# Both softmaxes moved ahead of the transposes' copies on ACT, in a top-k attention followed by a GELU MLP

## The chip, the core and the metric

The kernel runs on one core of a Trainium2 chip, in float32. The core has five engines, each with its own instruction queue that it works through in order: PE (matrix products and transposes through the identity), ACT (activations and copies out of PSUM), DVE (vector work, here the top-k search), POOL (elementwise work) and SP (issues DMAs). Matmul results go to PSUM, which has eight banks per partition; everything else lies in SBUF. An engine that reaches an instruction whose input is not there, or whose output buffer is still in use, stands still, and everything behind it in its queue stands too.

The metric is the device time of one execution in microseconds. Less is better.

## What is computed

For 8 batches of 8 heads with 576 positions of 64 elements: scores, the 32 largest of each row kept, softmax over them, product with v. The result, seen as 4608 tokens of 512 elements, goes through an MLP with an exact GELU (512 to 2048 to 512).

```python
scores = scale * np.matmul(q, k.transpose(0, 1, 3, 2))
kth = np.partition(scores, -top_k, axis=-1)[..., -top_k:-top_k + 1]
scores = np.where(scores >= kth, scores, -1000000000.0)
scores = scores - np.max(scores, axis=-1, keepdims=True)
attn = np.exp(scores)
attn = attn / (np.sum(attn, axis=-1, keepdims=True) + 1e-09)
attn_out = np.matmul(attn, v)
...
h = x @ w_in
g = 0.5 * h * (1.0 + erf(h * inv_sqrt2))
return g @ w_out
```

## The kernel before

**Items.** Two heads are a pair. The 576 positions of a head are four blocks of 128 and a tail of 64. An item is one block of 128 query positions of both heads of a pair; the tails of two pairs together are one item too (`t == NM` in the code). There are 18 items a batch, 144 in all (`N`), and two batches, 36 items, are one round of the schedule.

**The pipeline.** The main loop (L689) has one iteration per item and keeps four items at different stages. In iteration `n`:

- `scores(n + 2)` (L277): eight matmuls into the PSUM tile `s_ps` (L293), for the first 512 keys of each head; one more into `t_ps` (L298) for the last 64 keys of both heads; ACT copies them to the SBUF row tile `s` (L306, L309). Tail items use L315, L326, L332 and L335.
- `top_k(n)` (L341): on DVE, for each of two heads four rounds of MAX8 (L355, the eight largest) with a MATCH_REPLACE8 between rounds (L358, takes them out). `hooks` lets another step run inside; here `inverse(n - 1)` after the fourth round's MAX8.
- `threshold(n)` (L366): on POOL, two tiny steps (L370, L373) turn the top values into the two biases of the softmax.
- `softmax(n - 1, e)` (L390), `e` being the head: on ACT, a Prelu with a huge slope pushes everything under the 32nd value far down (L394), then Exp, with the row sum gathered into `den` (L395).
- `add_small(n - 1)` (L384): POOL adds 1e-9 to `den` (L387). `inverse(n - 1)` (L378): DVE takes the reciprocal (L381). `normalise(n - 1)` (L401): POOL multiplies both rows by it (L407), on five items DVE does it.
- `transposes(n - 2)` (L417): PE transposes the 512 main columns of both heads into two PSUM tiles `tp` (L436), ACT copies them to `pt` (L448). The returned `tails` transposes the last 64 columns of both heads (L453, L458) into the spare half of `t_ps`; its copy is L454 or L465.
- `attend(n - 3)` (L482): PE multiplies by v (L500, L511) once two blocks of a pair are transposed, that is in every other iteration, and for every tail item; it returns whether there was a product. ACT copies the product `o` to `xT`, the MLP's input (L505, L515, run by `copy_x`).

**The MLP** is cut into pieces, placed into PE's queue by `mlp(k)` (L638), which puts in up to `k` of them. An iteration has a quota of eight (`left`), four in iterations 10 and 11; a w_in piece is only taken when its tokens are finished (`ready`, set behind `scores`). A w_in piece is four matmuls into `h_ps` (L552); two units of them are followed by their GELUs on ACT (L563). A w_out piece is two matmuls into `y_ps` (L588), copied by ACT and stored by SP. Blocks of eight w_in pieces and of eight w_out pieces alternate, so an iteration has one or the other. What is left when the 144 items are through runs as one block at the end.

**PSUM.** The tag `tp` has two banks for which `tp` (twice), `t_ps`, the q/k transposes `tp_qk` and `o` take turns. `s_ps` is single, and takes two banks; `h_ps` and `y_ps` have two each.

**Other work in the loop.** The transposes of q and k of later pairs (`transpose_qk`, L234) come in pieces that are laid into fixed iterations (`prep_in`); the first piece also issues the next loads of q and k on SP. Up to iteration 18 the weights arrive as 16 units and are put together by ACT (`weights_size`) and POOL (`weights_add`, `weights_end`). Before iteration 10 (`START`) there is no MLP to do, and `keep_busy` puts idle matmuls into PE's queue.

**The order** is written by hand (`manual_schedule`): each engine's queue is the order in which the Python code emits its instructions. In the steady part (`late`) an iteration emits: `attend`, `copy_x`, one MLP piece (two without a product), the transposes of item n-2, scores and last keys of item n+2 with the tail transposes, softmax of head 0, one piece, two pieces, softmax of head 1, `add_small`, the q/k pieces, the other MLP pieces, GELUs, then search, threshold and normalise.

Of the kernel before, what the change touches and what calls it, by code (L numbers as in the profile page):

```python
# [14 lines left out]
def kernel(  # L15
# [169 lines left out]
    def waits(u):  # L185

        return u == ORDER[-1]
# [80 lines left out]
    def half(r, e):  # L268


        return slice((r ^ e) * TL, ((r ^ e) + 1) * TL)
# [2 lines left out]

        return spread(t[:, e * TL :], step + (TL if e == 0 else -TL), TL)

    def scores(i, tails=None):  # L277

        if i >= N:
            if tails:  # L280
                t_ps = ps.tile([P, 512], f32, tag="tp", name="t_ps")
                tails(t_ps)()
            return
        pair, t = items[i]
        S_of[i] = s = work.tile([P, 2 * S], f32, tag="s", bufs=5, name="s")
        s_ps = ps.tile([P, 2, 512], f32, tag="s", bufs=1, name="s_ps")
        if t < NM:
            qk = qk_of[pair]
            lhsT = qk[:, t * P : (t + 1) * P]
            for c in range(2):  # L290
                for e in range(2):
                    rows = slice(e * D, (e + 1) * D)
                    nc.tensor.matmul(  # L293
                        s_ps[:, e, c * 256 : (c + 1) * 256], lhsT=lhsT[rows, :],
                        rhs=qk[rows, KT + c * 256 : KT + (c + 1) * 256], start=True, stop=True,
                    )
            t_ps = ps.tile([P, 512], f32, tag="tp", name="t_ps")
            nc.tensor.matmul(t_ps[:, 0:P], lhsT=lhsT, rhs=qk[:, SM + P : KT], start=True, stop=True)  # L298
            copy_tails = tails(t_ps) if tails else None
            if i == 0:  # L300

                nc.scalar.activation(s[:, 0:SM], s_ps[:, 0], func=AF.Copy, scale=scale)
                nc.vector.tensor_scalar(s[:, SM : S + TL], t_ps[:, 0:P], scale, None, op0=ALU.mult)
                nc.scalar.activation(s[:, S + TL :], s_ps[:, 1], func=AF.Copy, scale=scale)  # L304
                return
            nc.scalar.activation(spread(s, S + TL, SM), s_ps, func=AF.Copy, scale=scale)  # L306
            if copy_tails:
                copy_tails()
            nc.scalar.activation(s[:, SM : S + TL], t_ps[:, 0:P], func=AF.Copy, scale=scale)  # L309
        else:  # L310
            t_ps = ps.tile([P, 512], f32, tag="tp", name="t_ps")
            for r in range(2):
                qk = qk_of[pair + r]
                for e in range(2):
                    nc.tensor.matmul(  # L315
                        t_ps[half(r, e), r * TL : (r + 1) * TL],
                        lhsT=qk[:, SM + e * TL : SM + (e + 1) * TL],
                        rhs=qk[:, SM + P + e * TL : SM + P + (e + 1) * TL],
                        start=True, stop=True,
                    )  # L320

            for r in range(2):
                qk = qk_of[pair + r]
                for e in range(2):
                    rows = slice(e * D, (e + 1) * D)
                    nc.tensor.matmul(  # L326
                        s_ps[half(r, e), r, :], lhsT=qk[rows, SM + e * TL : SM + (e + 1) * TL],
                        rhs=qk[rows, KT:], start=True, stop=True,
                    )
            copy_tails = tails(t_ps) if tails else None  # L330
            s2 = s.rearrange("p (r n) -> p r n", r=2)
            nc.scalar.activation(s2[:, :, 0:SM], s_ps, func=AF.Copy, scale=scale)  # L332
            if copy_tails:
                copy_tails()
            nc.scalar.activation(  # L335
                s2[:, :, SM:S], t_ps[:, 0:P].rearrange("p (r n) -> p r n", r=2),
                func=AF.Copy, scale=scale,
            )

    def top_k(i, hooks):  # L340


        stat_of[i] = st = {
            "top": work.tile([P, 2, TOPK], f32, tag="top", name="top"),
            "neg": work.tile([P, 2, 2], f32, tag="neg", name="neg"),
            "bias": work.tile([P, 2], f32, tag="bias", name="bias"),
            "den": work.tile([P, 2], f32, tag="den", name="den"),
            "rden": work.tile([P, 2], f32, tag="rden", name="rden"),
        }
        cur = [row(i, e) for e in range(2)]  # L350
        rest = work.tile([P, 2, S], f32, tag="rest", bufs=1, name="rest")
        n_op = 0
        for r in range(TOPK // 8):
            for e in range(2):
                nc.vector.max(st["top"][:, e, 8 * r : 8 * r + 8], cur[e])  # L355
            if r < TOPK // 8 - 1:
                for e in range(2):
                    nc.vector.match_replace(  # L358
                        rest[:, e], st["top"][:, e, 8 * r : 8 * r + 8], cur[e], LOWEST
                    )  # L360
                cur = [rest[:, e] for e in range(2)]
            if r in hooks:
                hooks.pop(r)()

    def threshold(i):

# [16 lines left out]
    def add_small(i):  # L383
        if i < 0 or i >= N:  # L384
            return
        st = stat_of[i]
        nc.gpsimd.tensor_scalar(st["den"], st["den"], 1e-9, None, op0=ALU.add)  # L387

    def softmax(i, e):

        if i < 0 or i >= N:
            return
        st, s = stat_of[i], row(i, e)
        nc.scalar.activation(s, s, func=AF.Prelu, bias=st["neg"][:, e, 1:2], scale=1.0, alpha=STEEP)  # L394
        nc.scalar.activation(  # L395
            s, s, func=AF.Exp, bias=st["bias"][:, e : e + 1], scale=1.0,
            accum_out=st["den"][:, e : e + 1],
        )
# [75 lines left out]
    def copy_x():  # L474
        while copies:
            copies.pop()()
# [161 lines left out]
    def mlp(n):  # L638
        for _ in range(n):
            if done[0] >= len(pieces) or pieces[done[0]][0] > ready[0] or left[0] == 0:  # L640
                return
            pieces[done[0]][1]()
            done[0] += 1
            left[0] -= 1
            if eager[0]:
                run_gelus()
# [22 lines left out]
    for pair in range(2):  # L669
        for piece in transpose_qk(pair, pair == 0):  # L670
            piece()
        if pair == 0:
            scores(0)
            scores(1)

# [11 lines left out]
    for n in range(ahead):  # L689

        left[0] = 4 if n in (START, START + 1) else 8
        eager[0] = n > N
        if not waits(unit_in(n)):
            weights_add(unit_in(n))
        product = attend(n - 3)
        late = n > START
        if not late:

            softmax(n - 1, 0)
        copy_x()  # L700
        if waits(unit_in(n)):
            weights_size(unit_in(n))
            weights_add(unit_in(n))
        if not (product and late and done[0] < len(pieces) and pieces[done[0]][0] > ready[0]):
            mlp(1)
            if not product:
                mlp(1)
        if n < START:

            keep_busy((4 if product or n == 0 else 14) * (1 if n < 5 else 2), ident)  # L710

        scores(n + 2, transposes(n - 2))
        ready[0] = n_tok[0]
        if late:
            softmax(n - 1, 0)
        mlp(1)
        if not late:
            softmax(n - 1, 1)
        prep = prep_in.pop(n, [])
        if n == START + 1:  # L720

            for piece in prep:
                piece()
            prep = []
        if n < START and product:
            keep_busy(5 if n < 5 else 10, ident)
        mlp(2)
        if late:
            softmax(n - 1, 1)
        add_small(n - 1)  # L730
        if ends_late(unit_in(n)):
            weights_end(unit_in(n))
        for piece in prep:
            piece()
            mlp(1)
        if n == 1:
            keep_busy(8, ident)

        run_gelus()
        mlp(left[0])  # L740
        run_gelus()
        if n < N:
            top_k(n, {3: lambda: inverse(n - 1)})
        else:
            inverse(n - 1)
        threshold(n)
        u = unit_in(n + 1)

        normalise(n - 1, 2 if on_pool(u) else 0)

        if not waits(unit_in(n + 1)):
            weights_size(unit_in(n + 1))
        for m in (n + 1, n + 2):

            if m > 2 and waits(unit_in(m)) == (m == n + 1):
                load_weights(m)
        if n <= NP:
            load("v", n)
# [38 lines left out]
```

## Time and profile before

| | us |
|---|---|
| median of three runs | 1755.2 (1753.03 to 1757.11) |
| the profiled execution | 1757.0 |
| its span, first to last instruction | 1755.2 |
| PE busy | 1618.2 (92%) |
| DVE busy | 1419.1 (81%) |
| ACT busy | 1173.6 (67%) |
| PE's weight loads busy | 1073.1 (61%) |
| POOL busy | 665.3 (38%) |
| first search starts / last reciprocal / closing MLP from | 10.3 / 1676.6 / 1689.3 |

The mean clock granted to PE was 0.982 of full speed. ACT loads its function tables 136 times, at 1.283 us each, about once for Exp and once for Gelu in two iterations.

How to read the lines below. A line of the timeline has the start in us, the length in us, the engine and source line, the operation, what it writes and reads, and how many instructions were merged; in square brackets stands the idle time of the engine before it, and who ended it. A line of the chain of waits in order of time has start, length and what. A line of the list of waits has who waited for whom, the total in us, how often, and the longest.

### The profile page before, as it was taken

Reading aid. Unit: us, or ns where it says so; the run is one execution under the profiler, and the core shown is the slowest. Engines: PE = TensorE matmul, PEld = TensorE weight load, DVE = VectorE, ACT = ScalarE, POOL = GpSimd, SP = SyncE. Lnnn points to the kernel's source line nnn. Section 1 sums busy time; section 2 is a strip of 40 time slices with the busy share of each in tenths; the row PEclk is TensorE's granted clock in tenths of the full one; section 3 lists DMA queues with packets and bytes.
Section 4 is the critical chain, followed back from the end, with each engine's and each line's share of the span. In section 5 each row is a group of like instructions: output and inputs, shape, how many; then the busy total and the mean of one; then the engine's idle time right before and its main releaser. Section 6 shows DMA issues by size and latency. Waiting matters only on the chain.

```text
span 1755.2 us, 28033 instructions
## 1 busy us (share of the span) xinstructions
PE 1618.2 (92%) x10336; PEld 1073.1 (61%) x10336; DVE 1419.1 (81%) x3046; ACT 1173.6 (67%) x2132; POOL 665.3 (38%) x760
## 2 busy tenths in 40 slices
PE   7778989999999999999999989999999999999999
PEld 6566566666656556666666556666666655666565
DVE  7888888888888778888888878888888878888800
ACT  6777876777767666677777767667676766666630
POOL 4775753333333323333333333333333323333300
PEclk9889999999999999999999999999999999999999
DMA  5422320011100110001100111001110001000000
GB/s 153 130 73 78 97 64 1 13 27 34 40 1 27 28 28 27 1 27 34 28 26 11 30 28 40 1 13 27 41 33 1 26 15 33 1 13 3 5 13 12
DMA packets 126777, 56.34 MB, mean 32 GB/s; under 512 B 117776, under 2 KB 118064, under 8 KB 126640
## 3 DMA queue, kind: packets, MB, share of 16 engines
q1 hardware_dynamic: 125376, 54.12, 11.5%
q8 instruction: 82, 1.34, 0.3%
q10 hardware_dynamic: 1200, 0.39, 0.1%
q14 instruction: 55, 0.45, 0.1%
q0 software_dynamic: 64, 0.03, 0.0%
HBM read 45.08 MB, written 9.44 MB: 31 GB/s over the span
## 4 chain that ended last, share of the span: by engine, by line
PE 49%; ACT 30%; POOL 18%; issue 2%; DMA 1%; SPq 0%; POOLq 0%; ACTq 0%; DVE 0%; DVEq 0%
PE y_ps L588 22%; POOL s L407 14%; ACT s L395 7%; PE o L500 7%; PE h_ps L552 6%; ACT s L394 6%; PE tp L436 5%; ACT L395 5%; ACT s L306 4%; ACT pt L448 4%; PE s_ps L293 4%; PE t_ps L298 1%; PE s_ps L326 1%; PE warm L666 1%; POOL neg L370 1%
## 5 line engine op out<-in xcount | busy, mean ns | idle before, releaser
L355 DVE MAX8 top<-rest 128x8 f32<-128x576 f32 x864 | 609.3, 747 | 0.0
L552 PE MATMUL h_ps<-xT,w_in_sb 128*128 128x256 f32 (+1 forms) x2560 | 535.0, 362 | 8.5 <-ACT g L563 8.5
L588 PE MATMUL y_ps<-w_out_sb,g 128*128 128x512 f32 x1152 | 528.7, 598 | 0.0
L552 PEld LDWEIGHTS h_ps<-xT,w_in_sb 128*128 128x128 f32 x2560 | 438.2, 191 | 73.8 <-issue 13.4
L407 POOL TENSOR_SCALAR s<-s,rden 128x576 f32<-128x576 f32 x278 | 476.4, 1723 | 0.6 <-DVE rden L381 0.4
L358 DVE MATCH_REPLACE8 rest<-top,rest 128x576 f32<-128x576 f32 x576 | 423.3, 742 | 0.0
L387 POOL TENSOR_SCALAR den<-den 128x2 f32<-128x2 f32 x144 | 32.0, 222 | 965.6 <-ACT s L395 965.6
L448 ACT COPY pt<-tp 128x512 f32<-128x512 f32 x256 | 137.4, 589 | 353.9 <-PE tp L436 353.9
L588 PEld LDWEIGHTS y_ps<-w_out_sb,g 128*128 128x128 f32 x1152 | 212.9, 193 | 198.2 <-issue 194.8
L395 ACT ACTIVATE s<-s,bias 128x576 f32<-128x576 f32 x288 | 223.3, 775 | 12.9 <-ACT s L394 0.4
L381 DVE RECIPROCAL rden<-den 128x2 f32<-128x2 f32 x144 | 23.8, 166 | 249.7 <-POOL den L387 249.7
L436 PE MATMUL tp<-ident,s 64*128 64x64 f32 x2304 | 128.0, 236 | 102.6 <-POOL s L407 95.5
L394 ACT ACTIVATE s<-s,neg 128x576 f32<-128x576 f32 x288 | 222.2, 772 | 0.0
L436 PEld LDWEIGHTS tp<-ident,s 64*128 64x128 f32 x2304 | 94.1, 141 | 192.8 <-POOL s L407 158.1
L358 DVE MATCH_REPLACE8 rest<-top,s 128x576 f32<-128x576 f32 x288 | 211.7, 743 | 0.0
L355 DVE MAX8 top<-s 128x8 f32<-128x576 f32 x288 | 201.8, 742 | 0.1
L500 PE MATMUL o<-pt,raw_v 128*64 128x256 f32 x1280 | 152.9, 386 | 0.8 <-ACT s L309 0.8
L293 PE MATMUL s_ps<-qk 64*128 64x256 f32 x1024 | 145.2, 404 | 1.4 <-ACT s L304 0.8
L500 PEld LDWEIGHTS o<-pt,raw_v 128*64 128x64 f32 x1280 | 86.6, 137 | 83.9 <-issue 40.6
L306 ACT ACTIVATE s<-s_ps 128x1024 f32<-128x1024 f32 x127 | 130.0, 1024 | 7.7 <-PE s_ps L293 7.4
L563 ACT ACTIVATE g<-h_ps 128x512 f32<-128x512 f32 x144 | 78.6, 595 | 37.8 <-PE h_ps L552 37.1
L293 PEld LDWEIGHTS s_ps<-qk 64*128 64x128 f32 x1024 | 92.4, 196 | 9.1 <-ACT s L304 1.0
(77 smaller groups left out, 1173.7 us busy)
## 6 DMA issues: line engine op xcount, KB each, us to landing
raw_q<-in_q_dram SPq DMA_DIRECT2D x64, 128.0 KB, 2.4
raw_v<-in_v_dram SPq DMA_DIRECT2D x64, 128.0 KB, 2.4
raw_k<-in_k_dram SPq DMA_DIRECT2D x62, 128.0 KB, 2.4
out_dram<-y SPq DMA_DIRECT2D x31, 256.0 KB, 2.2
w_out_sb<-in_moe_w_in_dram SPq DMA_DIRECT2D x14, 511.8 KB, 5.1
w_out_sb<-in_moe_w_out_dram SPq DMA_DIRECT2D x10, 511.8 KB, 4.1
words<-in_moe_w_out_dram SPq DMA_DIRECT2D x6, 511.8 KB, 4.3
out_dram<-y SPq DMA_DIRECT2D x9, 128.0 KB, 2.4
```

The source lines that it names most:

```text
L293: nc.tensor.matmul(s_ps[:, e, c * 256 : (c + 1) * 256], lhsT=lhsT[rows, :], rhs=qk[rows, KT + c * 256 : KT + (c + 1) * 256], start=True, s ...
L306: nc.scalar.activation(spread(s, S + TL, SM), s_ps, func=AF.Copy, scale=scale)
L355: nc.vector.max(st["top"][:, e, 8 * r : 8 * r + 8], cur[e])
L358: nc.vector.match_replace(rest[:, e], st["top"][:, e, 8 * r : 8 * r + 8], cur[e], LOWEST)
L394: nc.scalar.activation(s, s, func=AF.Prelu, bias=st["neg"][:, e, 1:2], scale=1.0, alpha=STEEP)
L395: nc.scalar.activation(s, s, func=AF.Exp, bias=st["bias"][:, e : e + 1], scale=1.0, accum_out=st["den"][:, e : e + 1],)
L407: (nc.vector if e >= 2 - on_dve else nc.gpsimd).tensor_scalar(s, s, st["rden"][:, e : e + 1], None, op0=ALU.mult)
L436: nc.tensor.transpose(tps[g][:, at : at + TL], s[rows, first[e] + j * P : first[e] + (j + 1) * P], ident[rows, rows],)
L448: nc.scalar.copy(out=dst, in_=src)
L500: nc.tensor.matmul(o[e * D : (e + 1) * D, 0:n], lhsT=vt[:, j, e, :], rhs=pt[:, e * NM + j if j < NM else 2 * NM, :], start=(j == 0), stop= ...
L552: nc.tensor.matmul(h_tile(u)[:, i, :], lhsT=w_in_sb[:, ko, f * P : (f + 1) * P], rhs=xT[:, ko, c0 : c0 + n], start=(ko == 0), stop=(ko == ...
L588: nc.tensor.matmul(y_of[sub], lhsT=g_of[u][:, i, sub * P : (sub + 1) * P], rhs=w_out_sb[:, f, :], start=(f == 0), stop=(f == FT - 1),)
```

## The change

It takes scores apart into `scores` (first 512 keys) and a new `last_keys` (last 64 keys, with the tail transposes of item n-2), and orders the iteration anew:

- `softmax(n - 1)` of both heads and `add_small(n - 1)` directly behind `copy_x`, ahead of the transposes
- one MLP piece ahead of the transposes with a product, three without
- behind the scores four MLP pieces, then `last_keys`
- a q/k piece comes behind an MLP piece instead of ahead of it
- the reciprocal behind the third round's MAX8 of the search, instead of the fourth's
- `normalise(n - 1)` ahead of `threshold(n)`

```diff
-    def scores(i, tails=None):
+    def scores(i):
...
-            t_ps = ps.tile([P, 512], f32, tag="tp", name="t_ps")
-            nc.tensor.matmul(t_ps[:, 0:P], lhsT=lhsT, rhs=qk[:, SM + P : KT], start=True, stop=True)
-            copy_tails = tails(t_ps) if tails else None
...
             nc.scalar.activation(spread(s, S + TL, SM), s_ps, func=AF.Copy, scale=scale)
-            if copy_tails:
-                copy_tails()
-            nc.scalar.activation(s[:, SM : S + TL], t_ps[:, 0:P], func=AF.Copy, scale=scale)
...
+    def last_keys(i, tails=None):
+
+        if i >= N and not tails:
+            return
+        t_ps = ps.tile([P, 512], f32, tag="tp", name="t_ps")
+        if i >= N:
+            tails(t_ps)()
+            return
+        pair, t = items[i]
+        s = S_of[i]
+        if t < NM:
+            qk = qk_of[pair]
+            nc.tensor.matmul(
+                t_ps[:, 0:P], lhsT=qk[:, t * P : (t + 1) * P], rhs=qk[:, SM + P : KT],
+                start=True, stop=True,
+            )
...
+        if tails:
+            tails(t_ps)()
+        if i == 0:
+            nc.vector.tensor_scalar(s[:, SM : S + TL], t_ps[:, 0:P], scale, None, op0=ALU.mult)
+        elif t < NM:
+            nc.scalar.activation(s[:, SM : S + TL], t_ps[:, 0:P], func=AF.Copy, scale=scale)
...
                 nc.vector.max(st["top"][:, e, 8 * r : 8 * r + 8], cur[e])
+            if r in hooks:
+                hooks.pop(r)()
             if r < TOPK // 8 - 1:
...
-            if r in hooks:
-                hooks.pop(r)()
...
         late = n > START
-        if not late:
-
-            softmax(n - 1, 0)
         copy_x()
+        for e in range(2):
+            softmax(n - 1, e)
+        add_small(n - 1)
         if waits(unit_in(n)):
             weights_size(unit_in(n))
             weights_add(unit_in(n))
-        if not (product and late and done[0] < len(pieces) and pieces[done[0]][0] > ready[0]):
-            mlp(1)
-            if not product:
-                mlp(1)
+        mlp(1 if product else 3)
...
-        scores(n + 2, transposes(n - 2))
+        tails = transposes(n - 2)
+        scores(n + 2)
         ready[0] = n_tok[0]
-        if late:
-            softmax(n - 1, 0)
-        mlp(1)
-        if not late:
-            softmax(n - 1, 1)
...
-        mlp(2)
-        if late:
-            softmax(n - 1, 1)
-        add_small(n - 1)
+        mlp(4)
+        last_keys(n + 2, tails)
         if ends_late(unit_in(n)):
             weights_end(unit_in(n))
         for piece in prep:
+            mlp(1)
             piece()
-            mlp(1)
...
+        u = unit_in(n + 1)
         if n < N:
-            top_k(n, {3: lambda: inverse(n - 1)})
+            top_k(n, {2: lambda: inverse(n - 1)})
         else:
             inverse(n - 1)
+
+        normalise(n - 1, 2 if on_pool(u) else 0)
         threshold(n)
-        u = unit_in(n + 1)
-
-        normalise(n - 1, 2 if on_pool(u) else 0)
```

More of the change, by code (lines that the diff above doesn't have):

```diff
@@ L275, in halves @@
         return spread(t[:, e * TL :], step + (TL if e == 0 else -TL), TL)
-    def scores(i, tails=None):
+    def scores(i):
         if i >= N:
-            if tails:
-                t_ps = ps.tile([P, 512], f32, tag="tp", name="t_ps")
-                tails(t_ps)()
             return
@@ L296, in scores @@
                     )
-            t_ps = ps.tile([P, 512], f32, tag="tp", name="t_ps")
-            nc.tensor.matmul(t_ps[:, 0:P], lhsT=lhsT, rhs=qk[:, SM + P : KT], start=True, stop=True)
-            copy_tails = tails(t_ps) if tails else None
             if i == 0:
                 nc.scalar.activation(s[:, 0:SM], s_ps[:, 0], func=AF.Copy, scale=scale)
-                nc.vector.tensor_scalar(s[:, SM : S + TL], t_ps[:, 0:P], scale, None, op0=ALU.mult)
                 nc.scalar.activation(s[:, S + TL :], s_ps[:, 1], func=AF.Copy, scale=scale)
@@ L306, in scores @@
             nc.scalar.activation(spread(s, S + TL, SM), s_ps, func=AF.Copy, scale=scale)
-            if copy_tails:
-                copy_tails()
-            nc.scalar.activation(s[:, SM : S + TL], t_ps[:, 0:P], func=AF.Copy, scale=scale)
-        else:
-            t_ps = ps.tile([P, 512], f32, tag="tp", name="t_ps")
+        else:
+            for r in range(2):
+                qk = qk_of[pair + r]
+                for e in range(2):
+                    rows = slice(e * D, (e + 1) * D)
+                    nc.tensor.matmul(
+                        s_ps[half(r, e), r, :], lhsT=qk[rows, SM + e * TL : SM + (e + 1) * TL],
+                        rhs=qk[rows, KT:], start=True, stop=True,
+                    )
+            s2 = s.rearrange("p (r n) -> p r n", r=2)
+            nc.scalar.activation(s2[:, :, 0:SM], s_ps, func=AF.Copy, scale=scale)
+    def last_keys(i, tails=None):
[9 more added lines that the diff above has]
+            qk = qk_of[pair]
+            nc.tensor.matmul(
+                t_ps[:, 0:P], lhsT=qk[:, t * P : (t + 1) * P], rhs=qk[:, SM + P : KT],
+                start=True, stop=True,
+            )
+        else:
             for r in range(2):
@@ L320, in scores @@
                     )
[L322 to L334, printed above, removed]
+        if tails:
[4 more added lines that the diff above has]
+            nc.scalar.activation(s[:, SM : S + TL], t_ps[:, 0:P], func=AF.Copy, scale=scale)
+        else:
             nc.scalar.activation(
-                s2[:, :, SM:S], t_ps[:, 0:P].rearrange("p (r n) -> p r n", r=2),
-                func=AF.Copy, scale=scale,
+                s.rearrange("p (r n) -> p r n", r=2)[:, :, SM:S],
+                t_ps[:, 0:P].rearrange("p (r n) -> p r n", r=2), func=AF.Copy, scale=scale,
             )
@@ L672 @@
         if pair == 0:
-            scores(0)
-            scores(1)
+            for i in range(2):
+                scores(i)
+                last_keys(i)
     slots_of = [
@@ L696 @@
         late = n > START
-        if not late:
-            softmax(n - 1, 0)
         copy_x()
+        for e in range(2):
+            softmax(n - 1, e)
+        add_small(n - 1)
         if waits(unit_in(n)):
```

## The prediction

> **What bounds the kernel now.** I read the chain of work that ended last first, because the shares of busy time leave two candidates (PE 92%, DVE 81%).
>
> ```profile
> PE 49%; ACT 30%; POOL 18%; issue 2%; DMA 1%; SPq 0%; POOLq 0%; ACTq 0%; DVE 0%; DVEq 0%
> ```
>
> The chain is shared by three engines: a loop between engines, not one full engine. Its pieces in order of time give the pace. These are three `normalise` pairs that lie 36 iterations apart, one round of the schedule:
>
> ```profile
> 259.11 3.42 POOL s L407 x2
> 673.02 3.42 POOL s L407 x2
> 1085.18 3.42 POOL s L407 x2
> ```
>
> So 36 iterations take 413.9 and 412.2 us, 413.3 on average (1085.18 to 1499.01 gives 413.8). The list of waits says who is held:
>
> ```profile
> DVE rden L381 <- POOL den L387: 249.7, 140, 12.6
> PE tp L436 <- POOL s L407: 95.5, 95, 4.2
> ```
>
> DVE stands 249.7 us at the reciprocal, PE 95.5 us at the transposes. Iterations come in two kinds. Call P one in which `attend` has a product, Q one without (in the steady part; five Ps follow each other around the tail items). The timeline of a Q, without the rows between:
>
> ```profile
> 806.99 0.17 DVE L381 RECIPROCAL rden<-den 128x2 f32<-128x2 f32 x1 [2.53 <-POOL den L387]
> 807.53 3.43 POOL L407 TENSOR_SCALAR s<-s,rden 128x576 f32<-128x576 f32 x2
> ...
> 811.01 0.46 PE L436 MATMUL tp<-ident,s 64*128 64x64 f32 x8 [1.24 <-POOL s L407]
> ...
> 811.50 1.07 ACT L448 COPY pt<-tp 128x512 f32<-128x512 f32 x2 [4.59 <-PE tp L436]
> ...
> 813.73 0.79 ACT L394 ACTIVATE s<-s,neg 128x576 f32<-128x576 f32 x1
> ...
> 816.86 0.19 ACT L395 ACTIVATION_READ_ACCUMULATOR s<-s,bias 128x1 f32 x1
> ...
> 817.13 0.22 POOL L387 TENSOR_SCALAR den<-den 128x2 f32<-128x2 f32 x1 [6.18 <-ACT s L395]
> 817.39 0.17 DVE L381 RECIPROCAL rden<-den 128x2 f32<-128x2 f32 x1 [0.59 <-POOL den L387]
> ```
>
> Here is the loop: reciprocal, POOL's normalise, PE's transposes, ACT's copies, the *next* item's softmax queued behind those copies, den, reciprocal: 817.39 - 806.99 = 10.40 us. In a P the loop has slack, and PE's own queue is what lasts:
>
> ```profile
> 818.44 2.38 PE L500 MATMUL o<-pt,raw_v 128*64 128x256 f32 x20
> 820.75 1.13 PE L552 MATMUL h_ps<-xT,w_in_sb 128*128 128x256 f32 x4
> 820.89 0.37 ACT L505 COPY xT<-o 128x256 f32<-128x256 f32 x1 [0.99 <-PE o L500]
> ...
> 821.81 0.71 PE L436 MATMUL tp<-ident,s 64*128 64x64 f32 x16
> 822.36 1.08 PE L293 MATMUL s_ps<-qk 64*128 64x256 f32 x8
> ...
> 824.78 0.79 ACT L394 ACTIVATE s<-s,neg 128x576 f32<-128x576 f32 x1
> ...
> 829.19 0.19 ACT L395 ACTIVATION_READ_ACCUMULATOR s<-s,bias 128x1 f32 x1
> ```
>
> **What the change removes.** Softmax(n-1) no longer stands behind the transposes' copies, the score copy and the tail copies. The loop becomes: reciprocal, normalise, threshold, softmax, den, reciprocal. Its price: reciprocal to end of normalise 0.17 + 3.43 and a little for signals, 3.6; threshold, now behind it, 0.45 (0.23 + 0.19 on L370, L373); softmax 3.32 (813.73 to 817.05), or 4.60 with a table load (824.78 to 829.38); den and signals to the reciprocal 0.35. That is 7.7 or 9.0 us. DVE alone needs 9.72 for a search (807.08 to 816.80) plus 0.23 for the reciprocal: 9.95. So the new loop is shorter than DVE's own work, and PE no longer stands in it. What is late next is PE's own queue.
>
> **PE's queue for 36 iterations**, by start-to-start times where nothing waits. An MLP piece is 4 w_in matmuls of 0.216 (16 take 826.84 to 830.29) or 2 w_out matmuls of 0.43: 0.863. 288 pieces: 248.5. Transposes 0.55 (821.81 to 822.36) x36: 19.8. Scores, last keys and tails 1.45 (822.36 to 823.81) less 0.1 waiting, x32: 43.2; for the four tail items 1.6 each: 6.4. Products 2.31 x16: 37.0, and four tail products at 1.4 (640 L511 matmuls, 22.2 us, over 16): 5.6. 80 q/k transposes of 0.11: 8.8. Sum 369.3. The diff moves pieces but issues the same ones: the quota of 8 an iteration stays, and `ready` is updated at the same point relative to the last chance to fill it, so 1096 of 1152 pieces are still done before the closing run of MLP, which costs what it did.
>
> **What it adds: waits on ACT's order.** Take a P from its start, 0. The copy of `o` starts at 2.45 (820.89 - 818.44) and ends at 2.8. Softmax with its load runs to 7.4, the reciprocal is possible at 7.75, the first copy of transposes is out at 8.0 and visible to PE at 8.2. PE reaches the last keys, which need that buffer, at 2.31 + 0.86 + 0.55 + 0.9 + 3.45 = 8.1. So it waits 0.1; without the four pieces it would wait 3.5. In a Q the softmax starts at the threshold, 4.1 after the P's reciprocal, 11.9, ends at 15.2, and the copies are out at 16.3; PE comes there at 11.1 + 2.6 + 0.55 + 0.9 + 3.45 = 18.6: no wait. Normalise for Q's transposes ends at 7.75 + 3.6 = 11.4, needed at 13.7: 2.3 of cover. For the next P: 17.7 + 3.6 = 21.3, needed at 23.
> Two cases cost. Where the Q before holds a q/k piece (11 of 18), its copy ends just ahead of the next P, and the gelus (load 1.28, two in 1.08) behind it end some 3.1 into the P: the first w_in piece waits about 0.5 and the softmax starts 0.6 late, 0.75 in all: 8.2. Where no piece is ready ahead of the transposes (some 5 Ps), PE comes 0.86 sooner to the last keys and waits about that: 4.3. Sum with the small ones 13: 369 + 13 = 382.
> The reciprocal on DVE now has two replaces and two MAX8 (2.8) behind it; if it is late, so are they, and the threshold on POOL behind them. It is ready at 7.75 of a P, and DVE reaches it about then (9.95 a turn, two turns 19.9 against PE's 20.5 to 21), so this hides behind PE. The threshold waits for normalise, 0.45 after it instead of before: inside the 7.7 to 9.0 above. The q/k loads on SP are issued one piece (0.86) later, two pairs ahead of use: nothing. add_small passes one weight step on POOL, once: nothing.
>
> **Ahead of the steady part** (before 245 us) an iteration takes about 12.2 against DVE's 9.95; POOL's weight adds (2.4 each) stand in the loop. New: 2.42 + 3.43 + 0.45 + 3.3 + den and signals 0.6 = 10.2 to 10.7. Eight such iterations save 13. Where POOL makes whole units (7.9 us each) I see no gain: 7.9 + 0.3 + 0.3 + 3.05 + 0.55 = 12.1, as now. Bounds 0 to -20.
>
> **Sum.** From 259 to the last reciprocal at 1676.8 there are 1417.7 / 413.3 = 3.43 rounds: 3.43 x (413.3 - 382) = 107. Profiled execution 1757.0 (span 1755.2) - 107 - 13 = 1637. That execution lies 1.8 above the median of 1755.2, so **1635**.
>
> **Two rules that say otherwise.** The row: a load makes the softmax 4.60 instead of 3.32, 1.28 more. The Trainium skill, page "ScalarE: Activation LUTs", section "What ACT_TABLE_LOAD costs", adds a drain of about 1380 ns to each switch; as an estimate by it, each pair would be 1.38 later, 25 a round, 407, and the kernel about 1720. The row: sixteen w_in matmuls follow each other at 0.216 without a gap, so PE is full there. The Trainium skill, "Perfetto Trace Analysis", section "Identifying the Most-Contended Engine", says to judge PE by weight-load busy time, here 61%; by that PE had headroom and only DVE's 36 x 9.95 = 358 would bound, about 1552. I go by the rows.
>
> **Rivals.** (1) *The softmax starts later than worked*: ACT's gelus and q/k copies in front of it are dearer. Everything in a P hangs on it, nearly one for one. With 0.9 us more a pair, 18 x 0.9 = 16 a round: 398, -52 - 13: 1690. For it: only 0.1 of cover at the last keys. Against: ACT is 67% busy and its order is known. (2) *Floor*: the stalls don't come: 373, -138 - 18: 1600. For it: PE's busy rows in a pair already hold little else. (3) *Slower: the transposes' buffers take over.* Both `tp` buffers stay full behind the softmax, and PE, in order, stands at the last keys in P and Q. It loses from 31/18 = 1.75 a pair beyond my sum; at 1.5 in each iteration, 54 a round against 31 won, +23 x 3.43 = 79 - 13: about 1820. Against: a Q has 2 us of cover. (4) *No change*: the threshold behind normalise makes the new loop as long as the old. It would need 2.4 more than 9.0 a turn; I find no row for that.
>
> **Chances.** Forecast 0.62 (own range 1600 to 1690, stalls of 4 to 26 a round, early part 0 to -20), rival 1 0.20, rival 2 0.06, rival 3 0.08, rival 4 0.04. A measurement of this kernel tells about 0.2% from no change. Faster 0.89, same 0.03, slower 0.08. The range reaches into rivals 1 and 2: 1598 to 1715.
>
> **What would show it.** After: the normalise pairs 36 iterations apart 382 apart; POOL's line nearly gone from the chain and PE above 75% of it; PE's wait for L407 under 20 us; a new PE wait of the last keys for ACT's `pt` copies of some 10 to 40 us; the reciprocal's wait down from 249.7 to some 100. Wrong if that new wait passes 100 us, or if the reciprocal's stays over 200.

## The result and the profile after

The changed kernel takes 1642.9 us (median of four runs, 1640.6 to 1645.0) against 1754.1 of the kernel before on the same chip: a ratio of 0.936, 95% interval 0.935 to 0.938. The forecast was 1635, range 1598 to 1715. The page of the changed kernel, busy times and chain:

```profile
span 1640.9 us, 27895 instructions
PE 1589.6 (97%) x10336; PEld 1059.6 (65%) x10336; DVE 1412.3 (86%) x3046; ACT 1179.4 (72%) x2132; POOL 665.4 (41%) x760
...
PE 84%; ACT 10%; POOL 3%; issue 1%; DMA 1%; SPq 0%; DVE 0%; ACTq 0%; DVEq 0%; POOLq 0%
```

The chain that ended last is now PE's own queue for 84% of the span (49% before). POOL's share, with normalise in it, fell from 18% to 3%. Three lines of the chain in order of time, 36 iterations apart (start, length, what):

```profile
276.49 3.65 PE h_ps L561 x16
663.46 3.65 PE h_ps L561 x16
1050.43 3.65 PE h_ps L561 x16
```

A round takes 387.0 us, 413.3 on average before. The list of waits (who for whom, total us, times, longest):

```profile
DVE rden L390 <- POOL den L396: 142.1, 71, 6.0
PEld h_ps L561 <- ACT g L572: 29.1, 48, 1.4
PEld tp L445 <- ACT xT L514: 15.0, 20, 1.9
PEld t_ps L323 <- ACT pt L457: 11.9, 8, 3.1
...
PE tp L445 <- POOL s L416: 0.6, 2, 0.4
```

PE's wait for normalise, 95.5 us before, is down to 0.6. DVE still stands at the reciprocal, 142.1 us in 71 iterations, mostly Ps. And there are small waits of PE and of its weight loads (PEld) for ACT; the one of the last keys (L323) for the `pt` copies lies wholly ahead of 240 us. A P with a q/k piece in the Q ahead of it, from its timeline:

```profile
764.50 2.38 PE L509 MATMUL o<-pt,raw_v 128*64 128x256 f32 x20
...
766.50 1.08 ACT L572 ACTIVATE g<-h_ps 128x512 f32<-128x512 f32 x2
...
767.14 1.13 PE L561 MATMUL h_ps<-xT,w_in_sb 128*128 128x256 f32 x4 [0.26 <-ACT g L572]
767.47 0.38 ACT L514 COPY xT<-o 128x256 f32<-128x256 f32 x1
767.72 0.80 ACT L403 ACTIVATE s<-s,neg 128x576 f32<-128x576 f32 x1
...
768.20 0.58 PEld L445 LDWEIGHTS tp<-ident,s 64*128 64x128 f32 x16 [0.33 <-issue]
...
769.77 3.32 PEld L561 LDWEIGHTS h_ps<-xT,w_in_sb 128*128 128x128 f32 x16 [0.33 <-issue]
...
772.23 1.05 ACT L457 COPY pt<-tp 128x512 f32<-128x512 f32 x2
...
772.67 0.17 DVE L390 RECIPROCAL rden<-den 128x2 f32<-128x2 f32 x1 [1.94 <-POOL den L396]
...
773.33 0.38 PE L323 MATMUL t_ps<-qk 128*128 128x128 f32 x2
```

The GELUs end 3.1 us into the P and the first w_in piece waits for them; the softmax runs from 3.2 (767.72) to the copies at 7.7 (772.23), the reciprocal comes at 8.2, and PE reaches the last keys at 8.8 without waiting. The prediction, with the 0.6 us that it gave such a P, had 3.1, 3.4, 8.0 and 8.35 for the first four.

Where the 114 us of span went: search 21 starts at 240.4 instead of 258.6 (18.2 won); searches 21 to 129, three rounds, take 1160.9 instead of 1239.9 (79.0); the rest 239.5 instead of 256.6 (17.1). Part of it may be PE's clock, for which the prediction has no term: by the clock records of the two traces PE is at half speed for 66 us before and for 26 us after, about half of the difference ahead of 250 us, and 40 us at half speed cost at most 20. No run separates that share.

### The profile page after: what moved, and what is told of

It reads as the page before. It is cut to its first block, busy times and chain, and to the rows that moved or that the text cites. A ratio compares the mean times of both kernels' runs of the same rounds, so it can differ in the third digit from the quotient of the medians.

```text
span 1640.9 us, 27895 instructions
## 1 busy us (share of the span) xinstructions
PE 1589.6 (97%) x10336; PEld 1059.6 (65%) x10336; DVE 1412.3 (86%) x3046; ACT 1179.4 (72%) x2132; POOL 665.4 (41%) x760
## 4 chain that ended last, share of the span: by engine, by line
PE 84%; ACT 10%; POOL 3%; issue 1%; DMA 1%; SPq 0%; DVE 0%; ACTq 0%; DVEq 0%; POOLq 0%
PE y_ps L597 31%; PE h_ps L561 31%; PE s_ps L290 6%; PE tp L445 5%; PE o L509 4%; ACT L572 3%; POOL s L416 2%; PE tp_qk L246 2%; PE t_ps L323 2%; ACT g L572 2%; ACT s L404 1%; ACT s L403 1%; PE s_ps L304 1%; PE t_ps L462 1%; ACT qk L250 1%
## 5 line engine op out<-in xcount | busy, mean ns | idle before, releaser
L561 PE MATMUL h_ps<-xT,w_in_sb 128*128 128x256 f32 (+1 forms) x2560 | 554.6, 365 | 10.1 <-ACT g L572 9.7
L597 PE MATMUL y_ps<-w_out_sb,g 128*128 128x512 f32 x1152 | 535.7, 599 | 0.0
L561 PEld LDWEIGHTS h_ps<-xT,w_in_sb 128*128 128x128 f32 x2560 | 434.7, 191 | 102.1 <-ACT g L572 29.1
L597 PEld LDWEIGHTS y_ps<-w_out_sb,g 128*128 128x128 f32 x1152 | 207.3, 190 | 206.9 <-issue 203.2
L390 DVE RECIPROCAL rden<-den 128x2 f32<-128x2 f32 x144 | 22.6, 157 | 142.4 <-POOL den L396 142.1
L445 PEld LDWEIGHTS tp<-ident,s 64*128 64x128 f32 x2304 | 86.0, 139 | 90.2 <-issue 69.2
L290 PE MATMUL s_ps<-qk 64*128 64x256 f32 x1024 | 139.6, 390 | 1.4 <-ACT s L296 0.8
L463 ACT COPY pt<-t_ps 128x128 f32<-128x128 f32 x128 | 34.5, 269 | 140.3 <-PE t_ps L462 139.9
L445 PE MATMUL tp<-ident,s 64*128 64x64 f32 x2304 | 109.0, 230 | 12.9 <-ACT xT L514 12.2
```

Source lines behind the costliest of these rows:

```text
L290: nc.tensor.matmul(s_ps[:, e, c * 256 : (c + 1) * 256], lhsT=lhsT[rows, :], rhs=qk[rows, KT + c * 256 : KT + (c + 1) * 256], start=True, s ...
L445: nc.tensor.transpose(tps[g][:, at : at + TL], s[rows, first[e] + j * P : first[e] + (j + 1) * P], ident[rows, rows],)
L561: nc.tensor.matmul(h_tile(u)[:, i, :], lhsT=w_in_sb[:, ko, f * P : (f + 1) * P], rhs=xT[:, ko, c0 : c0 + n], start=(ko == 0), stop=(ko == ...
L597: nc.tensor.matmul(y_of[sub], lhsT=g_of[u][:, i, sub * P : (sub + 1) * P], rhs=w_out_sb[:, f, :], start=(f == 0), stop=(f == FT - 1),)
```

## The experiments

All times in us. A round is the distance of searches 57 and 93 in the trace; "start" is where search 21 begins, the end of the part in which the weights are put together. Each ratio is against the kernel before, measured beside it.

| run | median | ratio, 95% interval | round | start |
|---|---|---|---|---|
| before | 1755 | | 412.2 | 258.6 |
| the change | 1642.9 | 0.936 (0.935 to 0.938) | 387.0 | 240.4 |
| recip_last | 1641.3 | 0.934 (0.931 to 0.937) | 387.0 | 236.4 |
| keys_early | 1967.7 | 1.119 (1.114 to 1.123) | 477.7 | 267.5 |
| softmax_late | 1683.3 | 0.958 (0.955 to 0.961) | 391.2 | 266.3 |
| hook_only | 1758.6 | 1.000 (0.998 to 1.002) | 409.8 | 278.3 |
| gelu_first | 1636.1 | 0.931 (0.930 to 0.933) | 385.2 | 239.3 |
| gelu_first_rec_last | 1632.6 | 0.930 (0.928 to 0.931) | 385.2 | 236.0 |
| three_pieces | 1656.9 | 0.943 (0.942 to 0.944) | 391.0 | 238.7 |
| two_pieces | 1712.0 | 0.975 (0.973 to 0.976) | 406.1 | 240.2 |
| third_piece_only | 1735.6 | 0.988 (0.986 to 0.991) | 405.9 | 263.3 |
| two_ahead | 1632.8 | 0.930 (0.927 to 0.932) | 383.8 | 239.6 |
| softmax_late_two_ahead | 1705.8 | 0.971 (0.969 to 0.974) | 396.5 | 266.2 |
| softmax_late_rec_last | 1704.1 | 0.970 (0.967 to 0.973) | 395.8 | 269.1 |

Theory A is the prediction's: the loop through PE bounded a Q, the softmax's new place takes PE out of it, the four pieces cover the wait for the PSUM bank, and then PE's own queue bounds.

### Which part of the change does the work

**recip_last**: the reciprocal's part undone.

```diff
-            top_k(n, {2: lambda: inverse(n - 1)})
+            top_k(n, {3: lambda: inverse(n - 1)})
...
-        normalise(n - 1, 2 if on_pool(u) else 0)
         threshold(n)
+        normalise(n - 1, 2 if on_pool(u) else 0)
```

> The changed kernel with the reciprocal back behind the fourth round's MAX8 and the threshold back ahead of normalise; softmax and last keys as changed. Theory A (the loop was cut by the softmax's place; PE's own queue bounds): the threshold then starts 0.5 us after the reciprocal instead of 4.1, normalise ends 4.1 after it instead of 3.6, still 1.8 us ahead of the transposes in a Q, so a round of 36 iterations stays at 387 us (383 to 391) and the time at 1643 (1630 to 1657). Rival B (the earlier reciprocal and normalise do the work): the transposes wait for normalise again by 1 us a pair or more, 405 a round or more, 1700 or more.

The round is the same to 0.1 us, so A's reading holds: once PE is out of the loop, nothing in the steady part hangs on when the reciprocal comes. The start is 4 us earlier, the part behind search 129 takes 2.6 us longer (242.1 against 239.5), and the intervals of the two ratios overlap: in the total no difference is shown.

**keys_early**: the cover undone.

```diff
         scores(n + 2)
+        last_keys(n + 2, tails)
...
         mlp(4)
-        last_keys(n + 2, tails)
```

> The changed kernel with the last keys and tail transposes directly behind the scores again, ahead of the four MLP pieces. Theory A (the transposes' PSUM bank comes free only behind the softmax, 8.2 us into a P, and the four pieces cover it): in a P PE comes to the last keys at 4.6 and waits 3.6 us; a Q has no wait. 18 x 3.4 = 61 a round more, 448, and about 1840 (1800 to 1880). The wait of t_ps for ACT's pt copies rises from 12 to some 200 us. Rival B (the bank is free early enough, the four pieces do nothing): 1643, 1630 to 1657.

Slower than before by 12%, and by more than A said (1800 to 1880). The timeline has the wait that A named, here 3.01 us (the line of PE), and the two rows of busy time by stage, of this kernel and of the changed one, have the rest (stretch, its length, then busy us and counts by engine, granted clock, DMA share, GB/s):

```profile
913.24 0.49 PE L323 MATMUL t_ps<-qk 128*128 128x128 f32 x2 [3.01 <-ACT pt L457]
```

```profile
734.91:1212.60 477.69, 415.33 (x2489) 276.35 (x2489) 352.34 (x757) 283.14 (x525) 145.89 (x181) 0.92 0.08 21
```

```profile
627.37:1014.34 386.97, 381.61 (x2490) 251.35 (x2489) 351.18 (x758) 285.60 (x525) 145.71 (x181) 1.00 0.10 26
```

PE's waits for pt copies sum to 57 us in this round, which makes 387 + 57 = 444, near the 448 expected. The other 34 go with the clock: its record has only full and half speed, so 0.92 on average means 2 x 0.08 x 477.7 = 76 us at half speed, which costs up to 38; PE is busy 34 us longer with the same instructions. This round is the dearest of the three: the ones on either side have the same 57 us of waits, a granted clock of 0.94 and 24 us more of busy PE than the changed kernel, and take 467.

**softmax_late**: only the softmax's place undone.

```diff
         copy_x()
-        for e in range(2):
-            softmax(n - 1, e)
-        add_small(n - 1)
...
         scores(n + 2)
+        for e in range(2):
+            softmax(n - 1, e)
+        add_small(n - 1)
```

> The changed kernel with both softmaxes and add_small behind the transposes' and scores' copies on ACT again; last keys four pieces later and the early reciprocal as changed. Theory A (the loop through PE is back, but is 0.45 us shorter without the threshold in it and 0.5 without the tail copies): in a P the softmax starts at 6.0, the reciprocal comes at 10.9, normalise ends at 14.5 and the Q's transposes, due at 13.7, wait 0.8 and those of the next P nothing: 8 to 18 a round more, 395 to 405, 1670 to 1705. Rival B (the softmax's place alone is the gain): the old loop of 10.4 us and 413 a round, 1735 or more. Rival C (its place does nothing): 1643, up to 1657.

The time lies where A had it, the round (391) a little under. So the softmax's place alone is *not* the steady gain: without it the other parts bring 21 of the 25 us of a round; its place brings 4 more, and 26 us ahead of search 21. The loop through PE is back but shorter. A Q of softmax_late, from its timeline:

```profile
739.35 0.17 DVE L390 RECIPROCAL rden<-den 128x2 f32<-128x2 f32 x1 [1.37 <-POOL den L396]
739.69 3.44 POOL L416 TENSOR_SCALAR s<-s,rden 128x576 f32<-128x576 f32 x2 [0.37 <-DVE rden L390]
...
743.20 0.71 PE L445 MATMUL tp<-ident,s 64*128 64x64 f32 x16
...
749.48 0.17 DVE L390 RECIPROCAL rden<-den 128x2 f32<-128x2 f32 x1 [0.32 <-POOL den L396]
```

10.1 us from reciprocal to reciprocal, and the transposes start just as normalise ends, at 743.1: PE has filled the time with the third piece. Most Qs take 9.86 and most Ps 11.14, the loop without and with the table load of 1.28; that is 21.0 a pair, under the 21.5 that the changed kernel takes (387.0 / 18). The loop is 0.54 shorter than the 10.40 before: 0.20 of it hook_only has too, and 0.34 is about what the tail copies took ahead of the softmax before (0.31, from 813.42 to 813.73). The later last keys, which take them out of its way, were not run alone.

**hook_only**: the kernel before with the reciprocal behind the third round and normalise ahead of the threshold (recip_last's edit, the other way, in the old kernel).

> The kernel before with one part of the change: the reciprocal behind the third round's MAX8 and normalise ahead of the threshold. Theory A: the loop of 10.40 us a Q loses the threshold's 0.45, 18 x 0.45 = 8 a round, 405, 1727 (1715 to 1740). Rival B (the reciprocal's place does the work): below 1690. Rival C (nothing): 1754, 1747 to 1761.

No difference, against A. Two effects cancel. A Q's loop is 10.20 instead of 10.40 (reciprocals at 818.26 and 828.46): A took the whole threshold (0.45) out of it, but normalise starts 0.34 behind the reciprocal (818.60) even with nothing between, instead of 0.54. That wins 2 to 4 a round. And the start is 20 us later. There the old kernel has one softmax ahead of the copies:

```profile
66.95 2.43 POOL L210 TENSOR_TENSOR w_in_sb<-w_in_sb,w_out_sb 128x1024 int32<-128x1024 int32 x1
...
69.36 3.44 POOL L407 TENSOR_SCALAR s<-s,rden 128x576 f32<-128x576 f32 x2
...
72.77 0.23 POOL L370 TENSOR_SCALAR neg<-top 128x4 f32<-128x4 f32 x1
...
73.03 0.78 ACT L394 ACTIVATE s<-s,neg 128x576 f32<-128x576 f32 x1 [2.98 <-POOL neg L370]
```

On POOL a weight add, then normalise, then the threshold, and ACT stands 2.98 us for it. The list of waits has this nine times, all ahead of 280 us, and in the kernel before not once:

```profile
ACT s L394 <- POOL neg L370: 23.5, 9, 3.0
```

### The third piece, the cover, and what is left

**third_piece_only**: the kernel before with `mlp(2 if late else 1)` for the second `mlp(1)` in an iteration without a product, that is three pieces ahead of a Q's transposes.

> The kernel before with one part of the change: three MLP pieces instead of two ahead of the transposes in a Q of the steady part. Theory D (PE in a Q only lacks work while normalise runs: the loop of 10.4 us starts afresh in each P, which has slack, so a piece put into the wait shortens the pair by its 0.86): 18 x 0.86 = 15 a round less, 398, 1702 (1690 to 1720). Theory A as I had it (the loop through PE bounds a Q whatever PE does meanwhile): 413 a round, 1754 (1745 to 1762).

Between the two ranges: 6 to 7 a round. The reciprocals of the timeline say why:

```profile
724.54 0.17 DVE L381 RECIPROCAL rden<-den 128x2 f32<-128x2 f32 x1 [0.59 <-POOL den L387]
736.22 0.17 DVE L381 RECIPROCAL rden<-den 128x2 f32<-128x2 f32 x1 [1.88 <-POOL den L387]
746.62 0.17 DVE L381 RECIPROCAL rden<-den 128x2 f32<-128x2 f32 x1 [0.59 <-POOL den L387]
758.29 0.17 DVE L381 RECIPROCAL rden<-den 128x2 f32<-128x2 f32 x1 [1.87 <-POOL den L387]
```

11.68 and 10.40 alternate. 10.40 is the loop of a Q, 11.68 the same with the table load of 1.28, of a P. Before, many Ps took 12.33, held by PE; with the piece moved they fall to the loop's 11.68, and there it ends. The loop binds both kinds: 22.08 a pair, or 397 for 18; the rest of the 406 lies mostly around the tail items, where Ps follow each other (10.8 to 13.2).

**two_ahead**: the changed kernel with `mlp(1 if product else 2)`.

> The changed kernel with two pieces instead of three ahead of the transposes in a Q, the third going behind the last keys. Theory A (with the softmax ahead, normalise ends 2.3 us before the transposes are due, 1.4 with a piece less): 387 a round, 1643 (1635 to 1652). Theory D in its strong form (the third piece is what gained): 387 + 15 = 402 a round, about 1695.

Faster than the change, by 10 us (the intervals of the ratios are apart), which is under A's range too. With the softmax ahead, a Q needs no third piece in front. Behind the last keys it does something: the weight loads' wait of h_ps for the GELU falls from 29.1 to 15.6 us. The likely reason is that a piece now stands behind the q/k transposes while ACT copies them and loads the GELU's table.

**softmax_late_two_ahead**: softmax_late and two_ahead together.

> softmax_late with two pieces instead of three ahead of a Q's transposes. There a round took 391 us with the loop through PE at about 9.9 to 10.2 and normalise ending as the transposes came due. Theory D: the cover is gone, 0.86 more in each pair, 391 + 15 = 406 a round, 1683 + 52 = 1735 (1720 to 1745). If not (rival: the later last keys alone bring softmax_late its 391): 1683 to 1695.

Between the two ranges: 5.3 a round more, not 15. As in third_piece_only, the piece in front is worth only what lies between PE's pace (396.5 / 18 = 22.0 a pair without it) and the loop's (9.86 and 11.14, 21.0 a pair). With the loop through PE it helps, without it it costs 3.

**softmax_late_rec_last**: softmax_late and recip_last together.

> softmax_late with the reciprocal behind the fourth round's MAX8 and the threshold ahead of normalise. In hook_only the other order saved 0.2 us of the loop in a Q and 3 to 4 a round, and cost some 15 to 20 us ahead of 260 us, where POOL's weight adds stand behind it. Expected: a round 391 + 0 to 4, the early part 15 to 20 shorter: 1663 to 1683. Rival (the early reciprocal carries the 391): 400 a round or more, 1700 or more.

The round is just above what was expected (+4.6, searches mostly 10.07 apart in a Q instead of 9.86), the time above it by 21 and in the rival's range: with the loop through PE the early reciprocal does count, though not with 9 a round. The start is not earlier, it is 3 us later. With both softmaxes behind the copies none stands waiting for the threshold (the lists of waits of both versions have no such row), so the cost seen in hook_only isn't there to be won. By the softmax's place alone softmax_late starts 26 us later than the change, and 8 later than the kernel before, which has one softmax ahead of the copies there; which wait makes these 26 was not traced.

**three_pieces** and **two_pieces**: `mlp(3)`, `mlp(2)` for `mlp(4)`.

> The changed kernel with three MLP pieces instead of four between scores and last keys (the fourth moves behind). Theory A (the bank comes free about 8.2 us into a P, when PE with four pieces arrives): a P waits 0.8 more, 18 x 0.8 = 14 a round, 401, 1690 (1675 to 1705), and PE's clock stays as it is. Rival B (some cover is left): 1643 to 1655.

> As three_pieces, with two. Theory A: a P waits 1.7 more, 30 a round, 417, 1745 (1725 to 1760). Theory C (waits of PE of about this length also bring stretches at half clock, as in keys_early, where stalls account for 57 us a round, and the granted clock of 0.92 for some 38 more): above 1760, with a mean granted clock under 0.98. Rival B: 1643 to 1680.

The first lies 2 us above rival B's range, the second between B's and A's; C did not come. The first piece taken away costs 4.0 a round, the second 15.1 more, 0.84 for each of 18 pairs, a whole piece. So the cover has some 0.6 to spare, where the working left nothing; this is an estimate, because the piece put behind pays something back as in two_ahead (the wait of h_ps for g is 15.5 and 11.0). PE's waits for the `pt` copies in two_pieces are 18 in a round, 1.0 us on average and 1.4 at most. The granted clock (the 1.00 in this row of two_pieces) stays up in the steady rounds of both versions, so these waits do not bring what 3 us brought in keys_early:

```profile
646.19:1052.28 406.09, 385.66 (x2489) 249.31 (x2489) 351.28 (x757) 287.02 (x525) 145.67 (x181) 1.00 0.10 24
```

**gelu_first**: `run_gelus()` also directly behind `last_keys`, ahead of the q/k pieces; **gelu_first_rec_last** with recip_last's edit on top.

> The changed kernel with the waiting GELUs put into ACT's queue ahead of the q/k pieces' copies (run_gelus() directly behind last_keys). Theory A (of the 17.7 us that a round of 387 has over PE's own 369.3, the w_in pieces that wait for the GELU's h_ps bank behind a q/k copy are a part: 29 us of weight-load waits in the whole run, 8 a round): 5 to 8 us a round less, 379 to 382, 1617 to 1628, and the wait of h_ps for g below 12 us. Rival B (the q/k copy is then what is late: the next P's product or transposes wait for its bank): 1643, 1638 to 1648.

> gelu_first, with the reciprocal behind the fourth round's MAX8 and the threshold ahead of normalise as in recip_last. Theory A (in the steady part nothing hangs on them; in the part ahead of 240 us the threshold behind normalise costs 4 us): gelu_first less 0 to 4 us. Rival B: with PE's queue shorter by 5 a round the reciprocal becomes the bound: slower than gelu_first by more than 5.

gelu_first lies between the two ranges, at 1.8 a round instead of 5 to 8. Both theories hold in part, as its list of waits shows:

```profile
PEld h_ps L561 <- ACT g L572: 13.7, 25, 1.4
...
PEld o L509 <- ACT qk L250: 7.7, 4, 1.9
```

Half of the GELU's wait is gone, and a new one of the product for the q/k copy takes part of it back. With the reciprocal last the start is 3 us earlier and the round the same, and the intervals of the two ratios overlap; that version and two_ahead are the fastest that ran, 1632.6 and 1632.8, each 0.6% under the change. The two together were not tried.

## Why the prediction was right

**The bound.** Right: a loop of 10.40 us before, PE's own queue after. third_piece_only shows the loop as a bound by itself (10.40 and 11.68, to 0.01), and in the change PE's wait for normalise is all but gone. The prediction saw the loop only in the Qs; it stood 0.65 or less under the Ps too.

**What cuts the loop.** Right for the change as a whole, too strong for the step that it named. It put the whole steady gain down to the softmax's place and gave no worth to the third piece in front, the earlier reciprocal and the last keys out of the softmax's way. softmax_late has these three without that place and reaches 391.2 of 412.2: the loop still goes through PE there, but at 21.0 a pair it is under PE's own pace. It was enough to shorten the loop so far; taking PE out of it brought 4 us a round. That forecast and result agree does not show the named step.

**The price of the new loop.** Right by consequence: in a steady round DVE waits at the reciprocal only in Ps, at 8.2 of a P where 7.75 to 8.35 was worked out. In a Q the search runs through: two_ahead's and the change's reciprocals there show no wait. DVE's own turn is 9.72 there, reciprocal included, where the prediction added 0.23 to that and had 9.95; nothing hung on it.

**The four pieces.** Right and needed: without them PE waits 3.0 (3.5 worked out). The prediction's slower rival was this wait. Its mechanism exists, with two differences: it sets in only when the cover goes, and then 20 times in a round of 36, not in P and Q alike; PE's clock then adds 24 to 34 us of a round to the 57 of waits. In the change itself the wait of the last keys that was forecast, 10 to 40 us, came to 9.3, ahead of 240 us.

**PE's queue: 382 predicted, 387.0 measured.** This sum is mis-sized in two terms, which partly cancel, so that it came so near is in part luck. The stalls were put at 13: 8.2 for Ps behind a q/k piece, 4.3 for Ps without a ready piece. The weight loads do wait in a round, 8.0 for the GELU, 3.8 of the product for the tails' copy, 2.9 of the transposes for the copy of `o`, 0.7 of the last keys for pt, but PE's matmuls still run meanwhile, and PE itself stands only 2.7, 2.3 and 0.2 us for the GELU, the copy of `o` and a q/k copy. Counted by the starts of PE's matmuls, with the ones that come late behind such a wait, the stalls cost about 7. So the Ps without a ready piece wait at the transposes, for the bank of `o`, and not at the last keys. Short was PE's own sum, 369.3, by about 11. It took each piece at the pace of matmuls that follow others of their kind, 0.216. Where one kind follows another, some 90 times in a round, PE loses 0.1 to 0.2 with no wait named. Behind the scores of the P above, the first w_in matmul starts 0.31 after the last score matmul, and the second 0.32 after the first. The rows of the weight loads show an idle 0.33 there (769.77, and 768.20 in front of the transposes) with no releaser. Before, the same 0.33 stood behind the scores 28 times in a round under the name of ACT's pt copy, which is why the prediction took scores, last keys and tails as 1.45 "less 0.1 waiting"; that is 3 of the 11.

**The early part: 13 predicted, 18 measured.** The iterations fell to DVE's own 9.8, under the 10.2 to 10.7 worked out, up to search 12. The ones in which POOL makes whole units are at 12.4 to 13.5, worked out as 12.1.

**What counted as nothing.** The reciprocal's earlier place: nothing in the steady part, as said. The early reciprocal and the threshold behind normalise together: some 4 us at the start, of which 2.6 come back at the end; the threshold was said to be within the loop. The q/k loads: PE waits for them twice at the start, 2.4 us in all against 2.7 before, and not later.

**The rules.** The Trainium skill, "ScalarE: Activation LUTs", section "What ACT_TABLE_LOAD costs", would have each switch cost about 2.66 us; third_piece_only has 11.68 against 10.40, 1.28 a switch, and the kernel came in at 1643, not 1720. The other rule of the prediction took weight-load busy time, one of two measures that its section names; it is 65% in the change, and yet PE is 84% of the chain and the kernel is not at 1552. The Trainium skill, "TensorE: Matmul & The Clock Gate", section "Part 1: The HAM clock gate", says that the clock goes by how busy PE was in windows of about 3.4 us; keys_early agrees in kind: its stretches at half speed in the steady rounds are 3.41 us long or a multiple, with 0.92 granted where PE stood 3.0 us in a P, and 1.00 where it stood about 1 (two_pieces). None of its waits in a round was as long as such a window; the longest is 3.32.

## What to carry to other kernels

When a chain of waits goes round through several engines, write the loop out with its durations and compare it with what each engine has to do by itself; moving one consumer ahead in an in-order queue can take whole engines out of the loop, and then the fullest queue sets the pace. The loop need not be cut for that: here it was nearly enough to shorten it below what the fullest queue takes, so try the parts one by one before giving one of them the credit. What was put ahead delays what stood there, so look for the buffer that is now held longer and put independent work between its producer and its next user: here four pieces of it decided between 6% faster and 12% slower. And once the loop is cut, try the other edits again one by one: the early reciprocal and the third piece helped while the loop was there; after it the first brought nothing and the second cost 3 us a round.

## What was not expected of the hardware

A stall of PE of 3.0 us in about every second iteration costs more than its length: in keys_early the granted clock fell to between 0.92 and 0.94, and 24 to 34 us of a round went to slower matmuls beside 57 us of waits. Waits of about 1 us in as many places (two_pieces) left the clock at 1.00. But two such waits close together may not: in the kernel before, each of the six stretches of 3.41 us at half speed between 250 and 1676 us lies beside a wait of 1.0 to 1.2 us for normalise and one of 0.7 us for a `pt` copy about 1 us later. Where the limit lies was not measured. And a row that names a releaser can name one that mattered little: the 0.33 us behind the scores.
